# Other landing times, transfer costs and issue times in the plan that orders a fused attention and MLP kernel

## The chip, the cores and the metric

The kernel runs on one core of one Trainium2 chip. A core has TensorE (PE, with its weight loads shown as PEld), VectorE (DVE), ScalarE (ACT), GpSimd (POOL) and SyncE (SP), and 16 DMA engines that all queues share. DMAs are issued from POOL, where the issue itself keeps the engine busy, and from SP. The metric is the device time of one execution in microseconds; lower is better.

## The reference

Eight batches of eight heads, 576 tokens, 64 columns a head. Attention is causal with a window of 64 tokens, and its output is the input of a two-layer MLP with a hard-swish between the layers:

```
scores = q @ k.T / sqrt(64)
mask = (rel >= 0) & (rel < 64)          # rel = query position - key position
attn = softmax(where(mask, scores, -1e9))
x = (attn @ v) as [4608 tokens, 512]
h = x @ w_in                            # [4608, 2048]
out = (h * clip(h + 3, 0, 6) / 6) @ w_out   # [4608, 512]
```

Inputs and output are float32; the kernel multiplies in bf16.

## The kernel before, in words

The 4608 tokens of all batches are cut into nine tiles of 512. For a tile t the first layer (`s1_part`, line 685) makes 16 blocks of hidden columns, each from four matmuls of 128x512, one for each pair of heads (`g` = 0 to 3). ACT and DVE turn a block into `gT` (lines 698 and 703). The second layer (`s2_part`, line 724) makes four output blocks of 128 tokens, each from 16 matmuls, and `s2_close` (line 737) copies and stores them. Attention of a batch makes the columns of `xT` that the next tiles need: tile 1 can't be finished in its first layer before batch 1's attention has written `xT`, tile 2 not before batch 2's, and so on. At the start of a tile a few blocks are begun with three of the four pairs of heads alone (`HEAD`, two blocks; `HEAD0`, four blocks in tile 0), so that the last pair of heads may come a little later.

Attention of a batch: batches 0 and 1 load q and k in a folded form with `load_cast` and fold them on PE (`fold_pair`, line 490); batches from 2 on load rows of q and k (`load_rows`: tiles `nq` and `nk`, three DMAs for each of five blocks of tokens) and turn them with one DMA transpose for q and one for k (`turn`, issued from SP, tiles `Tq` and `Tk`). V is loaded by `load_vhead` (batch 0) and `load_vrows` (five DMAs a batch); `shift_v` (line 433) then makes shifted copies inside the tile `V` on DVE, ACT or POOL. Scores are at line 529, the exponential at 545. The product with V is `pv` (line 626; LN at 632, EXP at 635, the product into `xT` at 646), or for some pairs of heads of batches 0 and 1 `pv_rows` (line 574; reciprocal at 584, product at 585) with a transpose `turn_x` (line 600) and a copy into `xT` (line 343).

All DMAs of POOL are one chain in a fixed order: batch 0's q and k, V heads, `w_in` (five DMAs), then `w_out` mixed with batch 1's q and k, V of batch 1, the rows of batch 2, and after that for each batch: its V, then the rows of the next. V of a batch from 2 on is held back by `hold`, a small POOL copy that reads `Tk` (line 801). Each queue uses eight semaphores in turn, so a DMA is not issued before the eighth one ahead of it has landed.

The order of the instructions on every engine is made by a planner (`Plan`) while the kernel is built. Every operation is an `Op` with an engine, or a choice of engines, and a duration. `solve` walks forward in planned time and takes, among the operations whose inputs are planned to be ready, the one with the earliest start after its rank and priority are subtracted. An operation that is not ready in the plan is passed over by one that is; on the chip each engine then runs the order as it stands, and waits where an input isn't there.

When an input is ready in the plan is, for a DMA, its planned landing. For the first six DMAs of SP and the first ten of POOL it is written out in `LANDED` (ns from the plan's start). For all others the planner works it out: a queue (`ring`) takes `packets * cost / 16` ns a DMA, plus 600 ns, plus `op.late`:

```
ring[eng] = self.landing(begin, op.packets, op.cost, seen["POOL" if eng == "SP" else "SP"])
op.done = max(op.land or ring[eng] + 600 + op.late, t + dur)
ring[eng] = max(ring[eng], op.done - 600 - op.late)
```

`late` is `LATER` for POOL's DMAs from the twelfth on and for the first two transposes (those of batch 2); it is 0 for the eleventh. `cost` is an argument of `dma`: 79 for `w_in` and `w_out`, 106 or 92 for `load_cast`, 14 for rows of q, k and V, 16 for `load_vhead`, 18 for the V rows that SP stages, 90 for a transpose. The time that POOL itself needs for an issue is `ISSUE[packets]`. The stream `main` (the MLP) keeps its own order on PE, and so does `att` (attention from batch 2 on); the operations of `pick` (attention of batches 0 and 1) may be taken in any order.

Of the kernel before, what the change touches and what calls it, by code (L numbers as in the profile page):

```python
# [20 lines left out]

WINDOW = 64
LANDED = {
    "SP": (2970, 3660, 6210, 7840, 8150, 10350),
    "POOL": (4550, 6480, 7920, 9200, 10360, 10930, 11370, 11790, 12210, 12680),
}
COLD_PE = 6500
FAR = 8.0e9
# [18 lines left out]
class Plan:  # L47
# [13 lines left out]
    def add(self, eng, dur, emit, reads=(), writes=(), prio=0, stream=None, after=(), alts=None, port=False):  # L61
        op = Op(eng, dur, emit, reads, writes, prio, stream or eng)
        op.alts = alts
        op.port = port
        for r in reads:
            if r in self.last_w:
                op.deps.add(self.last_w[r])
            self.readers.setdefault(r, []).append(op)
        for w in writes:
            if w in self.last_w:  # L70
                op.deps.add(self.last_w[w])
            op.deps.update(self.readers.get(w, ()))
            self.last_w[w], self.readers[w] = op, []
        op.follows = {a for a in after if a is not None}
        op.deps.discard(op)
        op.seq = len(self.ops)
        self.ops.append(op)
        return op
# [134 lines left out]
def kernel(  # L213
# [10 lines left out]
    P = nc.NUM_PARTITIONS  # L224
    B, H, S, D = q.shape
    DM, FF = moe_w_in.shape
    NT = B * S
    NG = H // 2
    assert D == 64 and NG * P == DM and WINDOW == D
    KB = (S + P - 1) // P  # L230
    SP = KB * P
# [31 lines left out]
    def sb(shape, dt, name):  # L263
        return consts.tile(shape, dt, name=name)
# [5 lines left out]
    A = {n: sb([P, NG, R, D], BF16, f"A{n}") for n in "qk"}  # L270
    N_ = {"q": sb([P, KB, NG, P], BF16, "nq"), "k": sb([P, NG, KB, P], BF16, "nk")}
# [26 lines left out]
    NT1 = 3  # L298
    HEAD = 2
    HEAD0 = 4  # L300
    LATER = 300
    IDLE = 96
    ROWS = (1, 2, 3)
    LATE = 13
# [18 lines left out]
    add = pl.add  # L323
# [34 lines left out]
        nst[0] += 1  # L358
        return i

    ISSUE = {P: 550, 2 * P: 700, 4 * P: 740, 8 * P: 880}

    def dma(packets, cost, out_ap, in_ap, reads=(), writes=(), stream="ld", after=(), kind="copy", eng="SP"):
        e = {"SP": nc.sync, "POOL": nc.gpsimd}[eng]
        if kind == "copy":
            em = lambda: e.dma_start(out=out_ap, in_=in_ap)  # L366
        else:
            em = lambda: e.dma_start_transpose(out=out_ap, in_=in_ap)
        op = add(eng, ISSUE[packets] if eng == "POOL" else 3300 if kind == "turn" else 500, em, reads=reads, writes=writes,
                 stream=stream if eng == "SP" else "issue", after=after)  # L370
        op.packets, op.cost = packets, cost
        return op
# [15 lines left out]
                [("stp", n, g)], [("A", n, g)] + st_keys(i, 0, NG, range(KB)), sbuf=True, prio=700)  # L388

    def load_cast(n, src, b, g0, g1, after=()):  # L390
        return dma((g1 - g0) * P, 106 if b == 0 else 92, A[n][:, g0:g1, :, :].rearrange("p g j d -> p g (j d)"),
                   src[b, 2 * g0 : 2 * g1].rearrange("(g h) (p j) d -> (h p) g (j d)", h=2, j=R),
                   writes=[("A", n, g) for g in range(g0, g1)], eng="POOL", after=after)

# [24 lines left out]
    def load_vrows(b, blk, after=()):  # L419

        s0 = blk * P if blk < NE else MAIN - D
        rows = slice(0 if blk < NE else D, P)
        to = V[rows, blk if blk < NE else 2 * NE - 1, :, :].rearrange("p g (t e) -> p (g t) e", e=2 * D)[:, :, 0:D]
        n = P - rows.start
        keys = [("V", g, 0, blk) for g in range(NG)] if blk < NE else [("V", g, 2, 2 * NE - 1) for g in range(NG)]
        return dma(n * H, 14, to, v[b, :, s0 + rows.start : s0 + P, :].rearrange("h s d -> s h d"), writes=keys, eng="POOL", after=after)

    def shift_v(g0, g1, engines, prio=0):
        vv = V[:, :, :, 0 : 3 * D].rearrange("p k g (t d) -> p k g t d", d=D)
# [39 lines left out]
    def turn(n):  # L469
        to = T_[n][:].rearrange("d (x s) -> d x s" if n == "q" else "d g (k s) -> d (g k) s", s=P)  # L470
        return dma(500, 90, to, N_[n][:].rearrange("p a b c -> p (a b c)"), reads=[("n" + n, kb, t) for kb in range(KB) for t in range(2)],
                   writes=[("T" + n, g) for g in range(NG)], kind="turn")
# [283 lines left out]
    def load_rows(b):  # L756
        for kb in range(KB):
            s0, ss = kb * P, min(P, S - kb * P)
            rows = slice(s0, s0 + ss)
            then(dma(ss * H, 14, N_["q"][0:ss, kb, :, :].rearrange("p g (t d) -> p (g t) d", d=D),  # L760
                     q[b, :, rows, :].rearrange("h s d -> s h d"), writes=[("nq", kb, 0), ("nq", kb, 1)], eng="POOL", after=chain))
            for t in range(2):
                then(dma(ss * NG, 14, N_["k"][0:ss, :, kb, t * D : (t + 1) * D],
                         k[b].rearrange("(g t) s d -> t s g d", t=2)[t, rows], writes=[("nk", kb, t)], eng="POOL", after=chain))
        turn("q")
        turn("k")
        then(hold("k", chain))
        load_v(b, range(KB))

    def load_v(b, blks):  # L770
        for blk in blks:
            then(load_vrows(b, blk, chain))
# [20 lines left out]
    def then(op):  # L793
        chain[0] = op
        return op
# [3 lines left out]
    def hold(n, after):  # L799

        return add("POOL", 100, lambda: nc.gpsimd.tensor_copy(out=scrap[:], in_=T_[n][:, 0:1] if n == "q" else T_[n][:, 0, 0:1]),  # L801
                   reads=[("T" + n, g) for g in range(NG)], writes=["scrap"], after=after)
# [4 lines left out]
        writes=["half", "m32"])  # L807
    add("DVE", 250, lambda: (nc.vector.memset(V[:, :, :, D : D + 2], 1.0), nc.vector.memset(V[:, :, :, 3 * D : 3 * D + 2], 1.0)),
        writes=["V1"])
    i0, iv = new_stage(), new_stage()  # L810
    load_pair("q", q, 0, 0, i0, 0)
    load_pair("k", k, 0, 0, i0, 1)
    load_tok(v, 0, iv, 0, 2, range(NE))
    then(load_cast("q", q, 0, 1, 2))
    then(load_cast("k", k, 0, 1, 2, after=chain))
    then(add("POOL", 600, lambda: make_identity(nc, ident32), writes=["c32"], after=chain))
    then(load_cast("q", q, 0, 2, 3, after=chain))
    then(load_cast("k", k, 0, 2, 3, after=chain))
    then(add("POOL", 900, mask_pool, writes=["m32"], after=chain))
# [7 lines left out]
    for e, times in LANDED.items():  # L827
# [3 lines left out]
        reads=["c32"], writes=["fold"], prio=3000)  # L831
# [16 lines left out]
    for g in range(0, NG, 2):  # L848
        for i in range(2):
            then(load_wout(g + i, after=chain))  # L850
        if g == 0:
            then(add("POOL", 1300, mask_pool16, reads=["m32"], writes=["mask"], after=chain))
        then(load_cast("q", q, 1, g, g + 2, after=chain))
        then(load_cast("k", k, 1, g, g + 2, after=chain))
        if g == 0:
            then(load_vrows(0, NE, chain))
    for n in "qk":
        then(add("POOL", pool(NG * P), lambda n=n: nc.gpsimd.memset(N_["q"][D:P, KB - 1, :, :] if n == "q" else N_["k"][D:P, :, KB - 1, :], 0.0),
             writes=[("n" + n, NE, 0), ("n" + n, NE, 1)], after=chain))
# [3 lines left out]
    for t in range(NTT):  # L863
# [23 lines left out]
        b = t + 1  # L887
# [19 lines left out]

    rank = {("PE", "att"): 300, ("PE", "pick"): 150, ("POOL", "issue"): 0, ("SP", "st"): 500}
    for o in [o for o in pl.ops if o.packets and o.eng == "POOL"][len(LANDED["POOL"]) + 1 :]:
        o.late = LATER  # L910
    for o in [o for o in pl.ops if o.packets and o.cost == 90][:2]:
        o.late = LATER
    order = pl.settle(rank, 8)
# [44 lines left out]
```

## Time and profile before

| | |
|---|---|
| Time, median of 3 runs | 303.61 us (303.5 to 304.5) |
| Profiled execution, its own time | 304.4 us |
| Its span, first to last instruction | 302.7 us |
| Granted TensorE clock | 1.00 |
| PE busy, share of the span | 289.8 us, 96% |
| ACT, DVE, POOL busy | 207.5, 199.6, 127.1 us |

A page of the profile groups instructions by line, engine and tile and gives busy time and waits. Times in its timeline and in its chain of waits count from the first instruction of the span. The plan's own clock starts at the first DMA issue of SP, which the trace has at 0.81 us. A time "in the plan" below is on the plan's clock and a time without that is the trace's. A busy PE is not a PE at its peak: matmuls overlap, and a shown duration is longer than the step from one matmul to the next.

### The profile page before, as it was taken

To read this page: it belongs to the slowest core of one execution; us is meant where nothing else is said; L and a number is where in the kernel's file an instruction comes from. 1 tells how busy PE (TensorE), PEld (TensorE's weight loads), DVE (VectorE), ACT (ScalarE), POOL (GpSimd) and SP (SyncE) were. 2 spreads that over 40 slices of the span, in tenths; PEclk is the share of its full clock that TensorE was granted. 3 is DMA by queue.
4 is the path that set the end of the run, shared out by engine and by line. 5 is a ranking of instruction groups with operands and counts; after the bars stand their busy time and mean duration, and the time that the engine had idled before them with its cause. 6 is when DMAs were issued, how large, how long until landed. Compare 5 with 4: busy or idle time off the path is not lost.

```text
span 302.7 us, 6789 instructions
## 1 busy us (share of the span) xinstructions
PE 289.8 (96%) x2703; PEld 154.5 (51%) x2749; DVE 199.6 (66%) x326; ACT 207.5 (69%) x323; POOL 127.1 (42%) x178
## 2 busy tenths in 40 slices
PE   7799998999999999999999999999999999999996
PEld 6544554445544454445587554455445544444443
DVE  3659737686578795788777885778678767206700
ACT  4768846678778785878678767877687858217711
POOL 8874769409920990496089229803200000000000
DMA  8999999999998999999999989948900010011011
GB/s 169 194 209 205 205 185 111 109 193 89 166 115 183 99 144 151 177 128 90 204 178 120 135 162 175 128 90 163 141 2 35 36 69 3 35 69 37 0 69 69
DMA packets 137760, 36.65 MB, mean 121 GB/s; under 512 B 126337, under 2 KB 132993, under 8 KB 137729
## 3 DMA queue, kind: packets, MB, share of 16 engines
q0 software_dynamic: 98896, 17.80, 73.0%
q1 hardware_dynamic: 38832, 18.42, 24.7%
q8 instruction: 21, 0.34, 0.5%
q14 instruction: 11, 0.08, 0.1%
HBM read 36.70 MB, written 9.44 MB: 152 GB/s over the span
## 4 chain that ended last, share of the span: by engine, by line
PE 77%; DMA 10%; POOL 6%; issue 4%; DVE 1%; ACT 0%; SPq 0%; POOLq 0%; DVEq 0%
PE pn L724 33%; PE pn L685 15%; PE pa L685 12%; PE pb L685 8%; DMA Ak<-in_k_dram 7%; PE pa L626 4%; POOL nk L366 2%; DMA Tk<-nk 2%; DMA V<-in_v_dram 1%; PE pa L529 1%; POOL V L433 1%; PE pa L724 1%; POOL nq L366 1%; POOL V L366 1%; PE pb L626 1%
## 5 line engine op out<-in xcount | busy, mean ns | idle before, releaser
L724 PE MATMUL pn<-wout,gT 128*128 128x512 bf16 x532 | 125.2, 379 | 2.1 <-issue 1.1
L685 PEld LDWEIGHTS <-win 128*128 128x128 bf16 x640 | 61.9, 98 | 60.8 <-issue 0.3
L724 PEld LDWEIGHTS <-gT 128*128 128x128 bf16 x592 | 54.1, 98 | 57.5
L685 PE MATMUL pn<-xT,win 128*128 128x512 bf16 (+1 forms) x274 | 63.2, 358 | 0.4
L703 DVE SCALAR_TENSOR_TENSOR gT<-t,pn 128x512 bf16<-128x512 bf16 x63 | 43.1, 686 | 11.1 <-ACT t L698 10.9
L698 ACT ACTIVATE t<-pn,half 128x512 bf16<-128x512 f32 x63 | 43.3, 689 | 9.9 <-PE pn L685 9.4
L685 PE MATMUL pa<-xT,win 128*128 128x512 bf16 (+1 forms) x202 | 48.0, 358 | 0.3
L703 DVE SCALAR_TENSOR_TENSOR gT<-t,pa 128x512 bf16<-128x512 bf16 x47 | 32.1, 687 | 23.7 <-ACT t L698 23.4
L366 POOL DMA_DIRECT2D nk<-in_k_dram x60 | 45.9, 812 | 1.2 <-DMA Ak<-in_k_dram 0.7
L698 ACT ACTIVATE t<-pa,half 128x512 bf16<-128x512 f32 x47 | 32.1, 687 | 8.6 <-PE pa L685 8.1
L646 DVE TENSOR_TENSOR xT<-pa,rec 64x512 bf16<-64x512 f32 (+1 forms) x48 | 32.5, 677 | 6.7 <-ACT rec L635 5.7
L685 PE MATMUL pb<-xT,win 128*128 128x512 bf16 (+1 forms) x149 | 35.3, 357 | 0.5 <-issue 0.5
L366 POOL DMA_DIRECT2D V<-in_v_dram x40 | 33.2, 853 | 4.7 <-PE pa L529 1.2
L703 DVE SCALAR_TENSOR_TENSOR gT<-t,pb 128x512 bf16<-128x512 bf16 x34 | 23.3, 687 | 16.3 <-ACT t L698 16.3
L737 ACT COPY osb<-pn 128x512 f32<-128x512 f32 x18 | 10.5, 585 | 33.5 <-PE pn L724 33.5
L632 ACT ACTIVATE rec<-pa 64x512 f32<-64x512 f32 (+1 forms) x48 | 27.9, 582 | 5.2 <-PE pa L626 4.1
L801 POOL COPY scrap<-Tk 128x1 bf16<-128x1 bf16 x6 | 1.1, 188 | 69.5 <-DMA Tk<-nk 69.5
L698 ACT ACTIVATE t<-pb,half 128x512 bf16<-128x512 f32 x34 | 23.4, 689 | 7.7 <-PE pb L685 7.7
L366 POOL DMA_DIRECT2D nq<-in_q_dram x30 | 27.6, 920 | 2.4 <-DMA wout<-in_moe_w_out_dram 1.6
L545 ACT ACTIVATE pT<-pa 128x1024 bf16<-128x1024 f32 x24 | 23.6, 1020 | 0.5 <-PE pa L529 0.5
L626 PEld LDWEIGHTS <-V 128*128 128x128 bf16 x464 | 17.5, 98 | 8.8 <-DVE xT L646 1.5
L554 DVE TENSOR_TENSOR pT<-pT,mask 128x1024 bf16<-128x1024 bf16 x28 | 19.1, 698 | 4.1 <-ACT pT L545 4.0
(88 smaller groups left out, 210.0 us busy)
## 6 DMA issues: line engine op xcount, KB each, us to landing
out_dram<-osb SPq DMA_DIRECT2D x35, 256.0 KB, 2.5
V<-in_v_dram POOLq DMA_DIRECT2D x28, 128.0 KB, 4.3
nq<-in_q_dram POOLq DMA_DIRECT2D x24, 128.0 KB, 4.1
nk<-in_k_dram POOLq DMA_DIRECT2D x48, 64.0 KB, 3.9
wout<-in_moe_w_out_dram POOLq DMA_DIRECT2D x4, 512.0 KB, 14.8
win<-in_moe_w_in_dram POOLq DMA_DIRECT2D x3, 512.0 KB, 9.8
V<-in_v_dram POOLq DMA_DIRECT2D x12, 64.0 KB, 5.6
Aq<-in_q_dram POOLq DMA_DIRECT2D x2, 288.0 KB, 14.0
```

The lines of the kernel that those rows point to most:

```text
L366: em = lambda: e.dma_start(out=out_ap, in_=in_ap)
L433: alts = {e: (c, (lambda e=e, rows=rows, src=src, k0=k0, n=n: cpy(e)(out=vv[rows, NE : NE + n, gs, 0:3:2, :], in_=vv[src, k0 : k0 + n, gs, ...
L545: nc.scalar.activation(out=p_[:].rearrange("p j h c -> p h j c"), in_=wide(add_far if masked else op, name)[:, :, 0 : n * D].rearrange("p ...
L554: nc.vector.tensor_tensor(out=pp, in0=pp, in1=mask[:, m0 : m0 + n, :, :].rearrange("p j h c -> p (j h c)"), op=MULT)
L626: nc.tensor.matmul(wide(op, name)[:, h, y * D : (y + 1) * D], lhsT=V[:, blk, g, h * D : h * D + P], rhs=p_[:, y, h, :], start=True, stop=True)
L632: add("ACT", act(n), lambda h=h: nc.scalar.activation(out=rc[rows[h], 0:n], in_=wide(op, name)[rows[1 - h], h, 0:n], func=LN), reads=[key] ...
L646: nc.vector.tensor_tensor(out=o, in0=a, in1=z, op=MULT)
L685: nc.tensor.matmul(bank(op, name)[:, to : to + n], lhsT=win16[:, g, fc * P : (fc + 1) * P], rhs=xT[:, g, o : o + n], start=(g == 0), stop= ...
L698: nc.scalar.activation(out=t1[ti][:], in_=bank(op, name), func=RELU, bias=half[:], scale=1.0 / 6.0)
L703: nc.vector.scalar_tensor_tensor(out=gT[:, fc, :], in0=t1[ti][:], scalar=1.0, in1=bank(op, name), op0=MIN, op1=MULT)
L724: nc.tensor.matmul(bank(op, name)[:, 0:n], lhsT=gT[:, fc, col : col + P], rhs=wout16[:, fc, js], start=(fc == 0), stop=(fc == NFC - 1))
L737: alts = {e: (f(n), (lambda e=e: cpy(e)(out=osb[oi][:, js], in_=bank(op, name)[:, 0:n])), False) for e, f in (("DVE", dve), ("ACT", act))}
```

## The change

Only numbers that the planner reads are changed. The operations and their shapes are the same, as are the buffers, the data and the order in the chain of POOL's DMAs.

- `LANDED`: new landing times for the first 6 DMAs of SP and the first 10 of POOL.
- `LATER` is 900 where it was 300, but for POOL's DMAs with a cost of 14 it stays at 300.
- The cost of rows is 16 where it was 14 for V of batches 0 and 1 and for q and k of batch 2, so these DMAs count as late by 900. V from batch 2 on, and rows of q and k from batch 3 on, keep 14 and 300.
- The cost of `load_cast` is 106 for batch 1 as well, where it was 92.
- POOL's issue of a DMA counts 740 ns whatever its size, where it was 550, 700, 740 or 880 by the number of packets.

```diff
 LANDED = {
-    "SP": (2970, 3660, 6210, 7840, 8150, 10350),
-    "POOL": (4550, 6480, 7920, 9200, 10360, 10930, 11370, 11790, 12210, 12680),
+    "SP": (2870, 3930, 6650, 7000, 8950, 10150),
+    "POOL": (5210, 6540, 8280, 9610, 10330, 12060, 12330, 12760, 13190, 13640),
 }
...
-    LATER = 300
+    LATER = 900
...
-    ISSUE = {P: 550, 2 * P: 700, 4 * P: 740, 8 * P: 880}
-
     def dma(packets, cost, out_ap, in_ap, reads=(), writes=(), stream="ld", after=(), kind="copy", eng="SP"):
...
-        op = add(eng, ISSUE[packets] if eng == "POOL" else 3300 if kind == "turn" else 500, em, reads=reads, writes=writes,
+        op = add(eng, 740 if eng == "POOL" else 3300 if kind == "turn" else 500, em, reads=reads, writes=writes,
...
     def load_cast(n, src, b, g0, g1, after=()):
-        return dma((g1 - g0) * P, 106 if b == 0 else 92, A[n][:, g0:g1, :, :].rearrange("p g j d -> p g (j d)"),
+        return dma((g1 - g0) * P, 106, A[n][:, g0:g1, :, :].rearrange("p g j d -> p g (j d)"),
...
     def load_vrows(b, blk, after=()):
...
-        return dma(n * H, 14, to, v[b, :, s0 + rows.start : s0 + P, :].rearrange("h s d -> s h d"), writes=keys, eng="POOL", after=after)
+        return dma(n * H, 16 if b < 2 else 14, to, v[b, :, s0 + rows.start : s0 + P, :].rearrange("h s d -> s h d"), writes=keys, eng="POOL", after=after)
...
     def load_rows(b):
...
-            then(dma(ss * H, 14, N_["q"][0:ss, kb, :, :].rearrange("p g (t d) -> p (g t) d", d=D),
+            then(dma(ss * H, 16 if b < 3 else 14, N_["q"][0:ss, kb, :, :].rearrange("p g (t d) -> p (g t) d", d=D),
...
-                then(dma(ss * NG, 14, N_["k"][0:ss, :, kb, t * D : (t + 1) * D],
+                then(dma(ss * NG, 16 if b < 3 else 14, N_["k"][0:ss, :, kb, t * D : (t + 1) * D],
...
     for o in [o for o in pl.ops if o.packets and o.eng == "POOL"][len(LANDED["POOL"]) + 1 :]:
-        o.late = LATER
+        o.late = LATER if o.cost != 14 else LATER // 3
     for o in [o for o in pl.ops if o.packets and o.cost == 90][:2]:
         o.late = LATER
```

## The prediction

> **What bounds the kernel now.** I read the page first, then who waited for whom on PE, then the chain of waits, then the timeline around each wait. Columns of the first fence: busy us, share of the span, instructions; then the chain's shares by engine.
>
> ```profile
> PE 289.8 (96%) x2703; PEld 154.5 (51%) x2749; DVE 199.6 (66%) x326; ACT 207.5 (69%) x323; POOL 127.1 (42%) x178
> PE 77%; DMA 10%; POOL 6%; issue 4%; DVE 1%; ACT 0%; SPq 0%; POOLq 0%; DVEq 0%
> ```
>
> PE sets the time: it is busy for 96%, and the number of matmuls doesn't change. What a new order can move is the time in which PE waits, and where the chain leaves PE it goes through DMA and POOL. PE's waits between 35 and 110 us (total us, times, longest):
>
> ```profile
> PE pb L574 <- POOL V L433: 0.8, 1, 0.8
> PE pb L626 <- POOL V L433: 0.7, 1, 0.7
> PE pa L626 <- DVE V L433: 0.3, 1, 0.3
> ```
>
> Each is a product with V that was put into PE's order before the shifted copy of V was there: batch 1, batch 2 and batch 3. They add up to 1.8 us. The chain of waits (start, us, what) leads there:
>
> ```profile
> 27.96 13.26 DMA Ak<-in_k_dram
> ...
> 49.18 0.96 POOL V L433
> ...
> 53.57 0.86 PE pn L724 x4
> ```
>
> Ak of batch 1 lands at 27.96 + 13.26 = 41.2 us, the copies of V follow, and PE waits for the one that ends at 49.18 + 0.96 = 50.1. Four matmuls take 0.86, so one takes 0.215 us; this is the coin in which the order is paid.
>
> **Planned against real landings.** Arithmetic on the plan's constants (a queue takes packets x cost / 16) gives the last V of batch 1. Before: 12.08 (the last written landing less 0.6), five w_in 10.30, four w_out 10.11, four casts of 256 packets at 92, 5.89, V of batch 0's end 0.45, V of batch 1 4.03: 42.9, with 0.6 and 0.3 behind it 43.8 in the plan, 44.6 in the trace's clock, in which the plan's start (SP's first issue) stands at 0.81. After: 13.04 to begin with (+0.96), casts at 106 (+0.90), V at 16 (+0.06 and +0.58), late by 0.9 in place of 0.3 (+0.6): 3.1 us more, 47.7. Real (SP's first issue; the last of batch 1's five V issues; then that one's KB and us to landing):
>
> ```profile
> 0.81 0.40 SPq L366 DMA_DIRECT2D stage<-in_q_dram  x1
> ```
>
> ```profile
> 36.34 0.69 POOL L366 DMA_DIRECT2D V<-in_v_dram  x1 [1.23 <-PE pa L529]
> ```
>
> ```profile
> V<-in_v_dram POOLq DMA_DIRECT2D x1, 64.0 KB, 9.2
> ```
>
> 36.34 + 9.2 = 45.5. The old plan is 0.9 us too early, the new one 2.2 too late. The order of POOL's DMAs is fixed, so I take the real landing as unchanged.
>
> **Part 1, the start (LANDED).** Rows:
>
> ```profile
> 5.53 6.77 DMA Ak<-in_k_dram
> 12.34 0.76 PE L490 MATMUL pn<-fold,Ak 64*64 64x64 bf16 x18 [0.19 <-DMA Ak<-in_k_dram]
> 12.42 0.62 ACT L343 CAST V<-stage 128x512 bf16<-128x512 f32 x1 [0.96 <-DMA stage<-in_v_dram]
> 13.63 0.45 PE L574 MATMUL pa<-V,pT 128*64 128x65 bf16 x16 [0.21 <-ACT Fq L495]
> 17.34 0.60 PE L685 MATMUL pn<-xT,win 128*128 128x512 bf16 x2
> ```
>
> The last k pair lands at 12.30, and the V that SP stages is there just as late (its cast starts at 12.42). The old plan has k at 10.93 and V at 10.35 plus a cast of about half a microsecond, so k is folded first (12.34) and the first product with V follows (13.63). The new one has k at 12.06 and V at 10.15: the two first products with V move ahead of the fold. On the chip the cast ends at 13.04, so the fold starts behind 13.04 plus two products of 0.45, less their overlap: about 13.6, 1.2 us later. But the first two pairs' x come 0.5 us sooner, and the blocks begun with three pairs (12 matmuls of 0.215, 2.6 us from 17.3 on) cover the last pair. Ends: -0.5 and +1.2; I take +0.3, nearest to the covered case.
>
> **Part 2, batch 1 (casts at 106, V at 16, late 900).** PE between the first product with V and tile 1:
>
> ```profile
> 46.80 0.69 PE L626 MATMUL pa<-pT,V 128*128 128x64 bf16 x16
> 48.13 1.04 PE L724 MATMUL pn<-wout,gT 128*128 128x512 bf16 x4
> 50.19 0.38 PE L574 MATMUL pb<-V,pT 128*64 128x65 bf16 x12 [0.83 <-POOL V L433]
> 51.92 0.45 PE L574 MATMUL pa<-V,pT 128*64 128x65 bf16 x16
> 52.30 1.04 PE L724 MATMUL pn<-wout,gT 128*128 128x512 bf16 x4
> 54.70 0.42 DVE L343 COPY xT<-pa 128x512 bf16<-128x512 bf16 x1 [0.30 <-PE pa L600]
> 56.66 0.38 PE L685 MATMUL pa<-xT,win 128*128 128x512 bf16 x1
> ```
>
> Some 20 second-layer matmuls of tile 0 (4.3 us) stand between these products in five groups of four. With V planned 3.1 us later about 14 of them (3.0 us) are put ahead: PE comes to the first product at 49.8, to the second row product near 51 and finds its copy done. The wait of 0.8 goes. What is late next is the last pair's x: the third row product waits for the last copy as before (about 52), 2.8 us of reciprocal, product, transpose and copy follow (51.92 to 55.12 now, 3.2), and only 6 matmuls (1.3 us) and the blocks begun with three pairs cover them. Now x is done at 55.12 and needed at 56.66, 1.5 us of room, so most of this fits. Ends: -1.0 (wait gone, chain covered) and +1.5 (a POOL issue, 0.74 to 0.89 a piece, goes ahead of the copies, and the tail is bare). I take -0.4.
>
> **Part 3, batch 2 (rows at 16, transposes and rows late 900).**
>
> ```profile
> 76.69 0.22 PE L626 MATMUL pb<-pT,V 128*128 128x64 bf16 x2
> 76.70 0.82 POOL L433 COPY V<-V 64x768 bf16<-64x768 bf16 x1
> 77.58 0.58 PE L626 MATMUL pb<-pT,V 128*128 128x64 bf16 x14 [0.67 <-POOL V L433]
> 82.16 0.52 PEld L626 LDWEIGHTS <-V 128*128 128x128 bf16 x16 [0.34 <-DVE xT L646]
> 87.01 1.39 DVE L646 TENSOR_TENSOR xT<-pa,rec 64x512 bf16<-64x512 f32 x2
> 88.82 0.38 PE L685 MATMUL pa<-xT,win 128*128 128x512 bf16 x1
> ```
>
> PE comes to the product at 76.69, goes on at 77.58 (0.83 lost behind the first two matmuls), and the last x is written at 88.40: 10.8 us for a chain whose third product waits until DVE has emptied a bank (82.16). x is needed at 88.82, so the room is 0.4 us. In the new plan everything of batch 2 follows V of batch 1 through POOL's eight semaphores (+3.1), plus 0.6 for its rows and 0.6 for its transposes, less a tile 1 that starts later in the plan too (3.1 less the 1.5 us of room): 4.3 - 1.6, about 2.7 us later against the MLP. Then PE has 2.7 us more of tile 1 ahead of the product: it comes there at 79.4, finds V (no wait, -0.8), and x is done at 79.4 + 10.8 = 90.2. Without the wait PE needs it at 88.0 and waits 2.2 us. Net +1.4. Ends: -0.8 (at most 1.2 us later, which wait and room swallow) and +2.2. I take +1.4, since the shift that I work out lies well past 1.2.
>
> SP: the store at 61.99 stands between the two transposes.
>
> ```profile
> 61.99 0.52 SPq L366 DMA_DIRECT2D out_dram<-osb  x1
> 62.80 3.16 SPq L368 DMA_TRANSPOSE Tk<-nk  x1
> ```
>
> With the transposes planned later the store may go ahead of both, and Tk is issued up to 0.8 sooner. V comes sooner by as much, but PE's order decides, so 0 (ends -0.4, the room, and +0.5, another store in between).
>
> **Part 4, batch 3 and behind, POOL's 740.** Landing rule and cost are unchanged there.
>
> ```profile
> 106.76 0.58 PE L626 MATMUL pa<-pT,V 128*128 128x64 bf16 x14 [0.27 <-DVE V L433]
> 115.47 2.81 DVE L646 TENSOR_TENSOR xT<-pa,rec 64x512 bf16<-64x512 f32 x4 [0.25 <-ACT rec L635]
> 120.59 0.38 PE L685 MATMUL pb<-xT,win 128*128 128x512 bf16 x1
> ```
>
> x is done at 118.28 and needed at 120.59, 2.3 us of room, and a PE that comes 0.3 later no longer waits for V: -0.3 (0 to -0.4). The flat 740 makes POOL's plan shorter by 0.14 for each 1024-row DMA, some 1 us a batch; the queue's 0.9 us a DMA hides it, and with that cover gone a batch's products would come 1 us too early in the order, a wait of up to 0.5. I take 0.
>
> **Sum.** 0.3 - 0.4 + 1.4 + 0 - 0.3 = +1.0 us. The profiled execution took 304.4 (span 302.7, 1.7 around it) and would take 305.4; it lies 0.8 over the median of 303.61, so I forecast 304.6.
>
> **A rule against the change.** DVE's copies of V move beside other issues of POOL.
>
> ```profile
> 75.64 1.27 DVE L433 COPY V<-V 64x1024 bf16<-64x1024 bf16 x2 [0.48 <-DMA V<-in_v_dram]
> 75.82 0.84 POOL L366 DMA_DIRECT2D nk<-in_k_dram  x1
> 77.47 0.74 POOL L366 DMA_DIRECT2D nk<-in_k_dram  x1
> ```
>
> The issue at 75.82 ran beside two DVE copies that ended at 76.91; it was done at 76.66, 0.10 longer than the one at 77.47 with no copy beside it. The Trainium skill (SBUF — State Buffer, the box on the "DVE blocks DMA" trap) says that a DVE copy in a two-port mode locks GpSimd out, so that descriptors wait for its end. By that rule the issue would have run past 76.91, and the trace disagrees. As a mechanism: where an issue ahead of V waits for one DVE copy of 0.65 us (half of 1.27), batch 2's V and its x come 0.65 later, and the time is 305.3.
>
> **Rivals.**
> - *Faster: the waits go and nothing takes their place.* If batch 2's products are put at most 1.2 us (five or six matmuls) later, wait and room swallow it: -0.8 there, -1.0 in batch 1, -0.4 in batch 3, 2.2 in all: 301.4; with half of it 302.5. For it: the old plan is early by 0.9 and all three waits are for V. Against it: the chain of 10.8 us with 0.4 of room.
> - *No change: the waits only move.* V lands by DMA and POOL alone, and what PE gains or loses in batch 1 is given back at batch 2's wait: 303.6, within 0.9. For it: the later wait absorbs an earlier loss of up to 0.8.
> - *Much slower: the start and batch 1's tail are bare too.* +1.2, +1.5, +1.4 less 0.8 that batch 2 absorbs, about +3: 306.7. For it: new landings 2.2 too late; against it: 1.5 us of room in tile 1.
> - *A DVE copy holds POOL* (the rule above): 305.3.
>
> **How the numbers follow.** Three runs of before spread over 303.5 to 304.5, so 0.3% (0.9 us) is about what a measurement tells from no change. Chances: slower by my sum, 304.0 to 305.9, 0.40; much slower 0.13; the DVE copy 0.02; no change 0.20; faster 0.25. Of the first case 0.05 lies within 0.9, so: faster 0.25, same 0.25, slower 0.50. The range takes half of the faster case and nearly all of the slower ones: 302.4 to 307.0. The likeliest case's own range is 304.0 to 305.9.
>
> **What would show it.** Right: PE's waits on V copies at 49 and 77 us are gone, and a wait of PE for xT (DVE, line 646) stands at the start of tile 2, near 88 to 90; at the start the first product with V stands ahead of the last fold; last V of batch 1 still lands near 45.5. Wrong: tile 2 starts without a wait (then the faster rival), V lands elsewhere because POOL's copies and issues changed places, or PE waits behind 120 us, where I expect nothing.

## The result and the profile after

The changed kernel is faster: 301.15 us median of 7 runs (300.86 to 303.01) against 303.54 of the kernel before (7 runs, 302.95 to 304.52); the ratio is 0.9926 with a 95% interval of 0.99 to 0.9952. The forecast was 304.6, the range 302.4 to 307.0. The profiled execution took 301.06 us, with a span of 299.4.

Lines of the changed kernel are two smaller: 722 is before's 724 (second layer), 683 is 685 (first layer), 624 and 572 are 626 and 574 (products with V), 431 is 433 (shifted copies of V). First its page, the lines that answer to those shown of before:

```profile
PE 292.4 (98%) x2749; PEld 154.3 (52%) x2749; DVE 198.2 (66%) x324; ACT 210.5 (70%) x329; POOL 124.6 (42%) x174
PE 94%; DMA 2%; ACT 1%; DVE 1%; SPq 0%; issue 0%
```

POOL has fallen out of the chain that ended last, DMA is down from 10% to 2%, and POOL has four instructions fewer: four copies of V have gone to ACT. PE's busy time is no measure here: the trace of before lacks records of 46 matmuls (2703 of 2749, while the weight loads, PEld, are 2749 in both). These are PE's waits over the whole run (total us, times, longest):

```profile
PE pn L917 <- DVE ones L804: 1.1, 1, 1.1
PE pa L488 <- DMA Ak<-in_k_dram: 0.9, 1, 0.9
PE pb L527 <- DVE Fk L493: 0.9, 1, 0.9
PE pn L598 <- DVE opg L583: 0.5, 1, 0.5
PE pb L572 <- ACT V L343: 0.3, 1, 0.3
```

All five lie ahead of 19 us, in the start. None is left for a shifted copy of V, in any batch, and none for x at the start of a tile.

To see where the time went I cut both timelines at four instructions: the first second-layer matmul (W, in tile 0) and the first matmul of tiles 1, 2 and 3 (T1, T2, T3). Rows of the timeline of before (start, us, what), with rows of POOL and SP that will be needed:

```profile
32.84 0.38 PE L724 MATMUL pn<-wout,gT 128*128 128x512 bf16 x1
...
46.35 2.08 POOL L433 COPY V<-V 64x384 bf16<-64x384 bf16 x3
...
49.18 2.18 POOL L433 COPY V<-V 64x384 bf16<-64x384 bf16 x3
...
55.08 1.29 POOL L366 DMA_DIRECT2D nk<-in_k_dram  x2
...
55.36 0.59 PE L685 MATMUL pa<-xT,win 128*128 128x512 bf16 x2
...
58.73 3.16 SPq L368 DMA_TRANSPOSE Tq<-nq  x1
...
87.53 0.81 PE L685 MATMUL pa<-xT,win 128*128 128x512 bf16 x3
...
119.30 0.81 PE L685 MATMUL pb<-xT,win 128*128 128x512 bf16 x3
```

The same of the changed kernel, with its copies and products in batches 1 and 2:

```profile
32.75 1.02 PE L722 MATMUL pn<-wout,gT 128*128 128x512 bf16 x4
...
46.27 1.70 POOL L431 COPY V<-V 64x512 bf16<-64x512 bf16 x2
...
46.69 1.34 ACT L431 COPY V<-V 64x384 bf16<-64x384 bf16 x3
...
48.05 0.63 PE L624 MATMUL pa<-pT,V 128*128 128x64 bf16 x16
48.62 0.45 PE L572 MATMUL pa<-V,pT 128*64 128x65 bf16 x16
48.89 0.42 PE L572 MATMUL pb<-V,pT 128*64 128x65 bf16 x16
...
52.95 1.28 POOL L364 DMA_DIRECT2D nk<-in_k_dram  x2
...
53.44 0.81 PE L683 MATMUL pn<-xT,win 128*128 128x512 bf16 x3
...
57.59 3.15 SPq L366 DMA_TRANSPOSE Tq<-nq  x1
...
73.12 0.95 POOL L364 DMA_DIRECT2D nq<-in_q_dram  x1
...
73.53 1.55 DVE L431 COPY V<-V 64x1024 bf16<-64x1024 bf16 x2 [0.17 <-DMA V<-in_v_dram]
...
74.89 0.63 PE L624 MATMUL pb<-pT,V 128*128 128x64 bf16 x16
...
84.76 0.81 PE L683 MATMUL pa<-xT,win 128*128 128x512 bf16 x3
...
115.96 0.81 PE L683 MATMUL pb<-xT,win 128*128 128x512 bf16 x3
```

From W to T1 the changed kernel needs 20.69 us in place of 22.52, from T1 to T2 31.32 in place of 32.17, from T2 to T3 31.20 in place of 31.77: 1.83, 0.85 and 0.57, together 3.25. W itself stands at the same place (32.75 and 32.84), which is chance, as the next section shows, and behind T3 the two traces agree to 0.01 us. So the gain is made in batch 1's attention, and again in batches 2 and 3. The profiled execution of before was 0.9 over its median, which is why the traces differ by 3.3 us and the medians by 2.4: part of the 3.25 belongs to that execution and not to the change. Run 9 below has before's order up to T1 and needs 22.20 us there, not 22.52, so where PE waits for V a stretch is known to some 0.3 us.

### The profile page after: what moved, and what is told of

It is laid out like the page before. It is cut to its first block, busy times and chain, and to the rows that moved or that the text cites. A ratio compares the mean times of both kernels' runs of the same rounds, so it can differ in the third digit from the quotient of the medians.

```text
span 299.4 us, 6829 instructions
## 1 busy us (share of the span) xinstructions
PE 292.4 (98%) x2749; PEld 154.3 (52%) x2749; DVE 198.2 (66%) x324; ACT 210.5 (70%) x329; POOL 124.6 (42%) x174
## 4 chain that ended last, share of the span: by engine, by line
PE 94%; DMA 2%; ACT 1%; DVE 1%; SPq 0%; issue 0%
PE pn L722 41%; PE pn L683 18%; PE pa L683 13%; PE pb L683 10%; PE pa L624 4%; PE pa L527 3%; DMA stage<-in_v_dram 2%; PE pa L722 1%; PE pb L527 1%; PE pb L624 1%; ACT pT L543 1%; PE pa L572 1%; PE pa L488 1%; DVE opg L583 0%; SPq L364 0%; PE pb L488 0%
## 5 line engine op out<-in xcount | busy, mean ns | idle before, releaser
L722 PE MATMUL pn<-wout,gT 128*128 128x512 bf16 x560 | 129.2, 379 | 0.0
L644 DVE TENSOR_TENSOR xT<-pa,rec 64x512 bf16<-64x512 f32 (+1 forms) x52 | 34.2, 658 | 9.5 <-ACT rec L633 8.5
L683 PE MATMUL pb<-xT,win 128*128 128x512 bf16 (+1 forms) x152 | 36.0, 357 | 0.0
L630 ACT ACTIVATE rec<-pa 64x512 f32<-64x512 f32 (+1 forms) x52 | 29.5, 567 | 6.6 <-PE pa L624 5.4
L735 ACT COPY osb<-pn 128x512 f32<-128x512 f32 x18 | 10.6, 586 | 31.4 <-PE pn L722 31.2
```

Of the source, the lines that this page charges most:

```text
L630: add("ACT", act(n), lambda h=h: nc.scalar.activation(out=rc[rows[h], 0:n], in_=wide(op, name)[rows[1 - h], h, 0:n], func=LN), reads=[key] ...
L644: nc.vector.tensor_tensor(out=o, in0=a, in1=z, op=MULT)
L683: nc.tensor.matmul(bank(op, name)[:, to : to + n], lhsT=win16[:, g, fc * P : (fc + 1) * P], rhs=xT[:, g, o : o + n], start=(g == 0), stop= ...
L722: nc.tensor.matmul(bank(op, name)[:, 0:n], lhsT=gT[:, fc, col : col + P], rhs=wout16[:, fc, js], start=(fc == 0), stop=(fc == NFC - 1))
L735: alts = {e: (f(n), (lambda e=e: cpy(e)(out=osb[oi][:, js], in_=bank(op, name)[:, 0:n])), False) for e, f in (("DVE", dve), ("ACT", act))}
```

## The experiments

An operation of the plan has a number (its place in the code). Most kernels here keep the finished plan and then move a few operations on their engine, or to another engine, by a function of my own, `settled(order, moves)`: a move takes numbers from their place and puts them behind another number on the named engine. The order of all other operations on each engine stays. Numbers: 165 and 172 to 177 are units of four second-layer matmuls of tile 0; 203 is the k fold of the third pair; 229 is the first product with V of batch 1, 235, 239 and 243 the row products, 237, 241 and 245 their transposes, 247 the last block; 209 to 216 are batch 1's copies of V and 350 to 353 those of batch 2; 268 is the first transpose of batch 2 and 181 the fourth store of tile 0. Lines in the rows of all these runs are numbered as in the kernel before.

W lies between 32.3 and 34.7 us in the 14 profiles of this study. The first loads move it (the sixth DMA of SP lands between 9.8 and 13.1 us), and so does the clock: between 9 and 16 us the granted clock was 0.52 in the profile of run 3 and 0.76 in those of runs 2 and 8. That jitter is one reason why times of kernels with equal stretches differ by some tenths.

The stretches are not free of it, since V doesn't land at a fixed distance from W. The last V of batch 1 lands 12.7 us behind W in the profile of before and 13.0 in that of the changed kernel, 11.8 to 13.2 in runs 1, 4, 6, 9, 11 and 12, but 10.6 to 11.7 in runs 2, 3, 5, 7, 8 and 10. In these six V had one to two us more to be in time, and a wait that is missing there may come back in other executions. The table has each run's stretches, and its times beside the kernel before on the same chip (303.94 us for the first four, 303.74 for the next, 304.0 for the last).

| kernel | W to T1 | T1 to T2 | T2 to T3 | median us | ratio, 95% interval |
|---|---|---|---|---|---|
| before | 22.52 | 32.17 | 31.77 | | |
| changed | 20.69 | 31.32 | 31.20 | 301.15 | 0.9926 (0.99 to 0.9952) |
| 1 before, PE's products moved | 21.65 | 32.80 | 31.55 | 303.3 | 0.9971 (0.995 to 0.9993) |
| 2 before, batch 1's copies moved | 22.13 | 31.34 | 31.20 | 303.11 | 0.9964 (0.995 to 0.9978) |
| 3 before, four moves | 21.63 | 31.21 | 31.20 | 302.22 | 0.9942 (0.9923 to 0.9962) |
| 4 changed, old LANDED | 20.68 | 31.32 | 31.21 | 301.09 | 0.9913 (0.9882 to 0.9944) |
| 5 changed, batch 1's copies back | 20.68 | 31.62 | 31.20 | 302.35 | 0.9953 (0.9935 to 0.9972) |
| 6 changed, PE's order back | 22.02 | 31.32 | 31.20 | 302.86 | 0.9984 (0.9955 to 1.0014) |
| 7 changed, SP's store back | 20.68 | 31.32 | 31.20 | 301.39 | 0.9924 (0.9901 to 0.9948) |
| 8 changed, batch 2's copies back | 20.68 | 31.45 | 31.20 | 301.83 | 0.9934 (0.9911 to 0.9958) |
| 9 before, batch 2's copies moved | 22.20 | 31.20 | 31.20 | 302.87 | 0.9969 (0.994 to 0.9997) |
| 10 before, all places of batch 1 | 21.04 | 31.20 | 31.20 | 301.61 | 0.9914 (0.9881 to 0.9947) |
| 11 before, late 900 alone | 21.03 | 32.60 | 31.39 | 302.82 | 0.996 (0.9945 to 0.9975) |
| 12 changed, late 300 | 20.90 | 31.61 | 31.20 | 301.61 | 0.9921 (0.9895 to 0.9948) |

**1. The products' place alone.**

```diff
     order = pl.settle(rank, 8)
+    order = settled(order, [("PE", [173, 174, 229, 235, 239, 175, 237, 176, 241, 243, 177, 247, 245], 172)])
```

> The kernel before, with one edit: on PE, the second-layer matmuls of tile 0 and batch 1's products with V stand in the order of the changed kernel (eight more second-layer matmuls ahead of the first product); every other engine and every copy of V as before. Theory A (two chains: PE's order in batch 1 and the arrival of batch 2's V must both move): the wait of 0.83 us near 50 is gone and tile 1 starts 0.8 to 1.8 us sooner, but V of batch 2 lands where it did (75.9), so PE's wait on V near 76 grows from 0.8 to 2 us or more and tile 2 starts at most 0.5 us sooner: 303.0 to 303.7 against 303.5. Theory B (the order of the products alone is the gain): tile 2 starts as much sooner as tile 1: 301.5 to 302.2.

Its timeline, POOL and PE in batch 1, then PE and POOL in batch 2:

```profile
48.75 0.50 POOL L433 COPY V<-V 64x384 bf16<-64x384 bf16 x1
...
48.93 0.76 PE L574 MATMUL pb<-V,pT 128*64 128x65 bf16 x16
...
54.07 0.81 PE L685 MATMUL pa<-xT,win 128*128 128x512 bf16 x3
...
75.44 0.22 PE L626 MATMUL pb<-pT,V 128*128 128x64 bf16 x2
...
76.04 0.82 POOL L433 COPY V<-V 64x768 bf16<-64x768 bf16 x1
...
76.92 0.58 PE L626 MATMUL pb<-pT,V 128*128 128x64 bf16 x14 [1.25 <-POOL V L433]
```

Theory A. Of the wait of 0.83 near 50 only a little is left (the row at 48.93 takes 0.76 where such a row takes 0.42 in the changed kernel), and the stretch to T1 is 0.87 shorter. The later product isn't all of it: PE comes to this row only 0.24 us later behind W than before, but the copy on POOL that it waits for takes 0.50 in place of 0.95; DVE's mask product, which ran beside it before, comes later here (see the last section). And PE now comes to batch 2 sooner, at 75.44, while V of batch 2 still goes through the copy on POOL that starts at 76.04: the wait grows from 0.67 to 1.25 (I had expected 2 or more), and 0.63 of the 0.87 is given back by T2.

**2. Batch 1's copies alone.** They take the engines that the changed kernel gives them.

```diff
+    order = settled(order, [("ACT", [210, 212, 214], 227), ("DVE", [213, 215], 226),
+                            ("POOL", [209, 211], 259), ("POOL", [216], 261)])
```

> The kernel before, with one edit: batch 1's eight shifted copies of V go to the engines that the changed kernel gives them (POOL 3, ACT 3, DVE 2 in place of POOL 6, DVE 2); PE's order as before. Theory A: the last copy ends about 1 us sooner, the wait of 0.83 us near 50 shrinks by at least half, and POOL issues the last rows of batch 2 about 1.5 us sooner (54.2 in place of 55.7), so V of batch 2 lands up to 1.1 us sooner and the wait near 77 goes too: 302.2 to 302.8. Theory B: the copies are not what counts; within 0.3 of 303.5.

```profile
48.55 0.57 PE L626 MATMUL pa<-pT,V 128*128 128x64 bf16 x14 [0.79 <-ACT V L433]
...
52.30 1.28 POOL L366 DMA_DIRECT2D nk<-in_k_dram  x2
55.39 3.20 SPq L368 DMA_TRANSPOSE Tq<-nq  x1
...
73.41 0.82 POOL L433 COPY V<-V 64x768 bf16<-64x768 bf16 x1
...
77.07 0.63 PE L626 MATMUL pb<-pT,V 128*128 128x64 bf16 x16
```

The part on batch 2 held: with three copies of V fewer in the way POOL issues its last two rows from 52.30 on in place of 55.08, the first transpose is issued at 55.39 in place of 58.73, V lands 2.7 us sooner, and PE's product at 77.07 doesn't wait, though POOL still makes one of its copies. In batch 1 I was wrong: the wait only moved, from a copy on POOL at 50 to one on ACT near 48, since PE's order asks for V ahead of time. The time fell by 0.8 us, the low end of what I expected.

**3. Both, with batch 2's copies and SP's store as in the changed kernel.**

```diff
+    order = settled(order, [  # the moves of the two kernels above, and
+        ("ACT", [351, 353], 330), ("DVE", [352], 350), ("SP", [181], 179)])
```

> The kernel before, with four edits: PE's order in batch 1 as in the first of these runs, batch 1's copies as in the second, batch 2's copies two on ACT and two on DVE (none on POOL), and SP's fourth store of tile 0 ahead of the first transpose. The start is as before. Theories A and B: 301.0 to 301.7, the time of the changed kernel, with tile 1 near 53.5, tile 2 near 84.8. Rival (the start, or the places of other small operations, carries the gain): above 302.2.

Batches 2 and 3 are now as short as in the changed kernel. The stretch to T1 isn't: 21.63 against 20.69, and the time is 302.22. By its number that is the rival's case: other places carry 0.94 us. Three rows of this trace say where 0.63 of it goes:

```profile
46.32 0.44 PE L529 MATMUL pa<-Fq,Fk 64*128 64x64 bf16 x18 [0.17 <-DVE Fk L495]
...
53.87 0.34 PE L600 MATMUL pb<-ident,opg 128*128 128x128 bf16 x3 [0.17 <-DVE opg L585]
...
56.13 0.40 PE L600 MATMUL pa<-ident,opg 128*128 128x128 bf16 x4 [0.29 <-DVE opg L585]
```

PE waits inside the scores for a folded k, and later twice for a normalized product: before's order on DVE puts the last mask product (0.68 us) between two normalizations.

**4. The start.** The changed kernel with the old numbers in `LANDED`:

```diff
-    "SP": (2870, 3930, 6650, 7000, 8950, 10150),
-    "POOL": (5210, 6540, 8280, 9610, 10330, 12060, 12330, 12760, 13190, 13640),
+    "SP": (2970, 3660, 6210, 7840, 8150, 10350),
+    "POOL": (4550, 6480, 7920, 9200, 10360, 10930, 11370, 11790, 12210, 12680),
```

> The changed kernel with the old LANDED times; the planner then gives the old start, and from tile 0's first block on the same order as the changed kernel. Theories A and B: the start is covered, 300.9 to 301.6 against 301.15 of the changed kernel. Rival (the new start gains or costs): more than 0.5 away; by my prediction's term of +0.3 for the new start, 300.85.

301.09, and the same stretches to 0.01 us. The new landing times of the start gain and cost nothing that can be seen here (each interval is about 0.3% to either side); the rival's 0.5 us or more isn't there.

**5 and 6. Taking one half of batch 1 back out of the changed kernel.** First the copies, then PE's order:

```diff
+    order = settled(order, [("POOL", [210, 212, 213], 259), ("POOL", [214, 215, 216], 260),
+                            ("DVE", [209], 226), ("DVE", [211], 228)])
```

> The changed kernel with batch 1's eight copies of V put back as before (POOL 6, DVE 2); PE's order and all else as in the changed kernel. The start of a run moves by a us or more with the first loads, so I read stretches: from the first second-layer matmul to tile 1 (20.7 us in the changed kernel, 22.5 before), and from tile 1 to tile 2 (31.3 and 32.2). Theory A (copies and PE's order are both needed): the fourth copy on POOL ends near 50, PE waits about 1 us in batch 1 (21.5 to 22.0), POOL issues its last row 2 us later (55.5), V of batch 2 lands near 75.5 and PE waits again in batch 2 (31.6 to 32.2): 302.2 to 303.2. Rival B (PE's order alone carries the gain): 20.7 and 31.3, 301.0 to 301.5.

```diff
+    order = settled(order, [("PE", [165], 203),
+        ("PE", [229, 235, 173, 239, 237, 174, 241, 243, 175, 247, 176, 245, 177], 172)])
```

> The changed kernel with PE's order in batch 1 put back: the third k fold ahead of four second-layer matmuls, and eight fewer of these ahead of the first product with V; the copies of V and all else as in the changed kernel. Theory A: the stretch to tile 1 grows from 20.7 to 21.5 to 22.0 us (PE waits for the copies of V and for the folded k), tile 1 to tile 2 stays at 31.3, since V of batch 2 comes no later: 301.9 to 302.5. Rival (taking the copies off POOL alone carries the gain): 20.7 to 21.0, 301.0 to 301.5.

With the copies back on POOL the stretch to T1 stays at 20.68: theory A's wait of about 1 us in batch 1 isn't in this profile. It is missing by a hair. POOL's fourth copy ends at 49.65, and the row that needs it began at 49.60 and took 0.49 in place of 0.42:

```profile
49.15 0.50 POOL L433 COPY V<-V 64x384 bf16<-64x384 bf16 x1
...
49.60 0.49 PE L574 MATMUL pb<-V,pT 128*64 128x65 bf16 x16
```

POOL's first copy starts 12.9 us behind W here and 13.5 in the changed kernel's profile. With POOL's copies 0.65 later, as there, PE would have waited some 0.7 us: an estimate from these rows. In batch 2 the copies cost 0.30 us, as theory A had it. Both together are about the 1.0 us by which this kernel's median stands above run 7's, but one profile can't show what the other executions lost.

With PE's order back the stretch to T1 grows by 1.33 to 22.02 (theory A), and one row of it says why: PE waits for a copy of V at once. The median, 302.86, is above theory A's range, and the interval of its ratio reaches 1.

```profile
46.94 0.57 PE L626 MATMUL pa<-pT,V 128*128 128x64 bf16 x14 [0.79 <-ACT V L433]
```

**7 and 8. SP's order and batch 2's copies, each put back in the changed kernel.**

```diff
+    order = settled(order, [("SP", [268], 179)])
```

> The changed kernel with SP's fourth store of tile 0 put back between the two transposes of batch 2. Theory A (SP's order carries nothing): the first transpose is issued up to 1.5 us sooner and the second about as before; PE doesn't wait in batch 2; 31.3 from tile 1 to tile 2, 300.8 to 301.5. Rival C (the store ahead of both transposes is what brings V of batch 2 in time): the second transpose is issued 0.8 us later or more, V lands at 74.7 or later, and PE waits 0.3 to 1 us: 301.5 to 302.2.

```diff
+    order = settled(order, [("ACT", [352], 330), ("POOL", [351], 400), ("DVE", [353], 350)])
```

> The changed kernel with batch 2's four copies of V put back as before: POOL 1, ACT 1, DVE 2. Theory A (POOL and V are early enough in batch 2 for any engine): 31.3 us from tile 1 to tile 2, no wait of PE on V: 300.8 to 301.5. Rival D (POOL's one copy of 0.82 us is the wait): PE waits 0.3 to 1.0 us behind two matmuls at 75: 31.6 to 32.2, 301.4 to 302.2.

SP's order carries nothing (theory A in both numbers). Run 8 is undecided. Its stretch of 31.45 lies between theory A (31.3) and rival D (31.6 or more), and its time of 301.83 is in D's range. POOL's copy is in time in this profile:

```profile
73.78 1.22 POOL L433 COPY V<-V 64x768 bf16<-64x768 bf16 x1
```

It is done at 75.00 and PE comes at 75.85. But V landed 18.6 us behind T1 here, against 20.5 in the changed kernel's own profile and 20.6 before; whether V is early enough for a copy on POOL in most executions isn't shown.

**9. Batch 2's copies alone.**

```diff
+    order = settled(order, [("ACT", [351, 353], 330), ("DVE", [352], 350)])
```

> The kernel before, with one edit: batch 2's four copies of V go two to ACT and two to DVE (before: POOL 1, ACT 1, DVE 2). Theory A2 (in batch 2 a V that lands about a us before PE comes is late for a copy on POOL and in time for ACT and DVE): from tile 1 to tile 2 31.3 to 31.6 us in place of 32.2, tile 2 to tile 3 as before or up to 0.5 shorter; the stretch from the first second-layer matmul to tile 1 stays at 22.1 to 22.5; 302.6 to 303.2. Rival E (V lands too late for any engine, only POOL's earlier issues cure it): 31.9 or more, 303.3 to 303.9.

Its timeline of batch 2 on ACT, DVE and PE, and T1 to T3:

```profile
54.72 0.38 PE L685 MATMUL pa<-xT,win 128*128 128x512 bf16 x1
...
74.49 1.56 ACT L433 COPY V<-V 64x768 bf16<-64x768 bf16 x2 [0.22 <-DMA V<-in_v_dram]
74.55 1.38 DVE L433 COPY V<-V 64x1024 bf16<-64x1024 bf16 x2
...
76.05 0.63 PE L626 MATMUL pb<-pT,V 128*128 128x64 bf16 x16
...
85.92 0.38 PE L685 MATMUL pa<-xT,win 128*128 128x512 bf16 x1
...
117.12 0.38 PE L685 MATMUL pb<-xT,win 128*128 128x512 bf16 x1
```

All four copies are done at 76.05 (74.49 + 1.56), just as PE comes, and PE doesn't wait; the first product needs only the first copy on each engine. V landed 20.1 us behind T1 here and 20.6 before, but these two were done at 75.32, 0.7 ahead of PE. T1 to T2 is 31.20 and T2 to T3 as well: taking one copy off POOL is worth all that batches 2 and 3 gained, 0.97 and 0.57 us in the traces. POOL's copy was late before because of POOL, not of V: V had landed at 75.94, and POOL went on with issues of batch 3's rows until 76.66 and only then to the copy (76.70). Batch 3 gains because that copy of 0.82 no longer stands in front of the rest of its rows: its first V is issued 9.9 us behind T2 (95.84 - 85.92) in place of 10.7 (98.23 - 87.53). So in batches 2 and 3 two edits do the same work, this one and the one of run 2, and either is enough.

**10. All places of batch 1.** The moves of run 3 without SP's, and with the k fold, the last mask product, and three small copies between DVE and ACT where the changed kernel has them:

```diff
+        ("PE", [203], 165), ("DVE", [228], 226), ("ACT", [178], 238), ("ACT", [246], 248), ("DVE", [180], 244)
```

> The kernel before, with its start and SP's order kept, and in batch 1 the places of the changed kernel for all that PE, ACT, DVE and POOL do behind the scores: the products with V, the third k fold, the eight copies of V, the last mask product ahead of the first normalization on DVE, two copies of results and one of x between DVE and ACT; and batch 2's copies of V on ACT and DVE. Theory A3 (batch 1's 1.8 us are the sum of small waits between PE, DVE and ACT, each gone by another place): 20.7 to 21.0 us to tile 1 and 31.2 to 31.4 to tile 2, 301.0 to 301.6. Rival (something else carries the 0.9 us that the run with four edits left, such as the start or SP): 21.4 or more, 301.8 to 302.4.

21.04 and 31.20, 301.61 us: theory A3, at the upper end of its ranges. What is still missing of batch 1's 1.83 is 0.35, and it is one wait: the scores with three pairs wait for a folded k in this kernel (0.71 us from their first to the next scores, 0.36 in the changed one). DVE copies that half of k here, from 45.05 to 45.81, and starts only behind ACT's copy of the other half (44.28 to 44.92); in the changed kernel the two engines are exchanged and the copies overlap (from 42.76 and from 43.04). No run exchanged these two alone.

```profile
45.86 0.44 PE L529 MATMUL pa<-Fq,Fk 64*128 64x64 bf16 x18 [0.18 <-DVE Fk L495]
```

**11 and 12. The constant `LATER`.** Alone in the kernel before, and taken back in the changed one:

```diff
-    LATER = 300
+    LATER = 900
...
-        o.late = LATER
+        o.late = LATER if o.cost != 14 else LATER // 3
```

> The kernel before, with one constant of the plan changed: late 900 in place of 300 (300 for POOL's transfers of cost 14). PE's order in batch 1 then differs from before by one unit of four matmuls and one fold, POOL keeps five of batch 1's copies and one of batch 2's. Theory (the later landing of batch 1's V comes from the costs and the order of issues, hardly from late): 21.8 to 22.5 us to tile 1, 31.5 to 32.4 to tile 2, 303.0 to 303.9. Rival (late is what moves the plan): 20.7 and 31.3, 301.0 to 301.6.

> The changed kernel with late 300 again everywhere; PE's order behind the start stays almost that of the changed kernel, POOL has three of batch 1's copies and one of batch 2's. Theory (late isn't needed): 20.7 to 20.9 us to tile 1, 31.3 to 31.6 to tile 2, 300.9 to 301.6. Rival (late carries the gain): 302.5 or more.

Rows of q, k and V keep 300 in run 11, since all have a cost of 14 there. The constant isn't needed for most of the gain: without it 20.90, 31.61 and 301.61, 0.5 us more in the stretches. Alone it did more in batch 1 than I expected, 21.03; the k fold is copied by exchanged engines, as in the changed kernel, and POOL has five copies of V in place of six, without an issue between them, but which of these it is wasn't taken apart. Batch 2 gives 0.43 back (32.60), with a wait of 0.71 for the copy on POOL, as in run 1. The other constants, the costs and POOL's 740, were not run alone: the runs show which places make the gain, not which constant makes each place. No run here was faster than the changed kernel by more than the intervals, and none of the remaining waits behind the start is worth a tenth of a per cent.

## Why the prediction was wrong

**Part 3, batch 2, is the step that failed**: +1.4 was forecast, -0.85 came. The step was "about 2.7 us later against the MLP". PE came to batch 2's first product 21.33 us behind T1 before (76.69 - 55.36) and 21.45 after (74.89 - 53.44): no later. The order on PE is the same in both kernels from tile 1 on. A later landing in the plan shifts an order only if it was the last input in the plan, and here the plan had room. The plans that the two kernels make have V of batch 2 2.4 us later, not 4.3, and tile 1 1.0 later, not 1.6; the first product is 1.2 later, so 0.2 against the MLP, where 2.7 was forecast. In both plans the product waits for a copy that stands on DVE behind a mask product until 73.7 and 74.9, and the V that it copies is planned for 72.0 and 74.4: room of 1.7 us, of which 0.6 is left. The chain of 10.8 us and the room of 0.4 us at T2 were read rightly, but nothing pressed on them. What ended the wait was something the step held fixed: which engine makes the copies (run 9), and how soon POOL gets to the rows (run 2).

**"The order of POOL's DMAs is fixed, so I take the real landing as unchanged"** held for batch 1's V (45.5 before, 45.8 after) and failed for batch 2's: it landed at 73.90 in place of 75.94. Behind T1 that is 20.5 in place of 20.6 us, so V came sooner by as much as PE did. The order of the DMAs is fixed, the copies between them are not. This step also hid the coupling that run 1 shows: had V of batch 2 landed as before, the gain of batch 1 would have come back as a wait.

**Part 2, batch 1**: -0.4 was forecast, -1.83 came, outside its ends (-1.0 and +1.5). Right: the wait of 0.83 goes, and second-layer matmuls go ahead of the first product (eight, not 14: in the plan the product is 3.1 us later, but the second layer itself is 1.4 later, and the step counted all of the 3.1). Wrong: "the tail" cost nothing, and terms were missing. Runs 1, 3 and 10 take the sum apart: 0.87 the products' place, 0.6 the places of the k fold, the last mask product and small copies, and what is left, 0.35, stands at the copies of a folded k. Runs 3 and 10 had V one to two us sooner behind W, so the shares are good to some 0.3 us. Beside the one wait for V, each of these is made of waits of 0.3 us or less, which I hadn't priced.

**Part 1, the start**: the order changed as forecast, a first product with V ahead of the last fold. The term of +0.3 isn't seen: run 4 is at the changed kernel's time.

**Part 4 and SP**: batch 3 gained 0.57 where 0.3 (to 0.4) was forecast. The wait that goes was the right one, the reason was not, so the sign is luck: PE doesn't come later (18.74 us behind T2 in both), V comes sooner (its last landing is 17.3 us behind T2 in place of 18.2), which depends on POOL's copy in batch 2. The store's place was taken at 0, and run 7 says 0.

**The rivals.** The faster one happened: the waits went and nothing took their place. Its reason was only half right: it had products at most 1.2 us later and the old room swallowing that, 301.4; they came 0.1 later and the rest was made by earlier copies. That its 301.4 is so near is luck: it has 1.0, 0.8 and 0.4 for the three batches, and the traces 1.83, 0.85 and 0.57. The rival of no change had the coupling of run 1 right, but not that copies and rows would come sooner too.

The DVE copy that holds POOL didn't appear: POOL's issue at 73.12 was done at 74.07, while DVE's copies of batch 2's V ran from 73.53 to 74.32 and to 75.08, and V was in time. By the rule of the Trainium skill (SBUF — State Buffer, the box on the "DVE blocks DMA" trap) an issue with descriptors still to be written at 73.53 would have waited for the end of that copy, at 74.32. This issue, which had begun before the copy, ended 0.25 sooner. The prediction took the row of before at 75.82 as against the rule, and that was misread: the first of the two DVE copies beside it ended at 76.15, and the issue ran until 76.66. In these traces no issue that began while such a copy ran on DVE ended ahead of it, so they don't refute the rule. What is longer here is DVE's copy: it takes 0.42 where POOL does nothing beside it, and 0.79 and 0.83 beside these issues.

## What to carry to other kernels

A copy that a busy engine waits for should not stand on the engine that issues transfers in order. It comes only behind the issues ahead of it (here 0.8 us after V had landed), and it holds up those behind it by its own time, a price that is paid a batch later. A gain on one engine's order is kept only if the next chain comes sooner by as much, so a wait that goes has to be followed to the next place where the two chains meet. And when planning constants change, work out whether the moved time was the last input of anything in the plan before shifting the order by it; to compare two traces, cut them at the same instructions, since the start alone jitters by more than such a change is worth, and look how far the transfers are ahead at each cut, since a wait can be missing for the jitter's sake alone.

## What was not expected of the hardware

A store of 256 KB between row loads may delay these loads. In the changed kernel two stores are issued from 51.65 on, in run 7 one; batch 2's last block of q rows, issued at 52.27 and 52.23, takes this long to land (out<-in, KB, us; first the changed kernel, then run 7):

```profile
nq<-in_q_dram POOLq DMA_DIRECT2D x1, 64.0 KB, 5.2
```

```profile
nq<-in_q_dram POOLq DMA_DIRECT2D x1, 64.0 KB, 3.8
```

In the changed kernel the first transpose is issued 1.4 us later than in run 7 (57.59 against 56.16), and that costs nothing only because PE doesn't wait in batch 2. How much of the delay is the second store's isn't shown: run 8 has the changed order on SP too, with the stores at 52.61 and 54.74, and there the same block took 4.1 us and the first transpose was issued at 56.45.

POOL's copy of 64x384 takes about twice as long when it starts beside a mask product that is running on DVE. Before, the one at 49.18 took 0.95 us, beside a mask product on DVE that ran from 49.09 to 49.77; in the changed kernel the one at 49.46 had only a normalization out of PSUM beside it and took 0.50:

```profile
49.09 0.68 DVE L554 TENSOR_TENSOR pT<-pT,mask 128x1024 bf16<-128x1024 bf16 x1
...
49.18 0.95 POOL L433 COPY V<-V 64x384 bf16<-64x384 bf16 x1
```

```profile
49.46 0.50 POOL L431 COPY V<-V 64x384 bf16<-64x384 bf16 x1
```

If the copy starts first, DVE is the longer one: before, POOL's copy at 46.35 took 0.50, and the mask product that began at 46.45 took 0.94 in place of 0.68. The same copy on ACT took about 0.5 three times. What the two engines share was not tried.

The granted clock of TensorE can fall in the start alone. In the profile of run 3 it was 0.52 between 9 and 16 us and 1.00 from 16 to 33, and W stands at 34.74 there. Of the eight executions of run 8, the four with a mean granted clock of 0.994 took 302.1 to 303.4 us, and the four with 1.00 took 301.2 to 301.6.
